# Column sums of the gates by products with ones, and an earlier hand-over from plain to seven-product units

## Chip, cores, metric

One core of one Trainium2 chip. The metric is the time of one execution in microseconds on the device; lower is better. The core has TensorE (PE, matrix products; PEld is its weight load), VectorE (DVE), ScalarE (ACT), GpSimd (POOL) and SyncE (SP, which issues the transfers here). Each engine works its own instructions off in program order; semaphores join them.

## What is computed

```
x  = attention(q, k, v)                      # windowed and dilated heads, to (2304, 512)
P  = exp(x @ w_gate - max)                   # (2304, 8)
for _ in range(8):                           # Sinkhorn
    P /= P.sum(1, keepdims=True) + 1e-9      # over the 8 experts
    P /= P.sum(0, keepdims=True) + 1e-9      # over all 2304 tokens
    P *= 2304 / 8
for e in range(8):
    out += P[:, e:e+1] * (relu(x @ w1[e]) @ w2[e])     # 512 -> 1024 -> 512
h = out @ w_in                               # 512 -> 2048
g = where(h >= 1, h, where(h <= -1, 0, (h + 1)**2 / 4))
return g @ w_out
```

## The kernel before, in words

All factors of the large products are split into a high part (rounded by an ACT copy) and a low part (raw minus high, a DVE subtraction): `split`, lines 98 and 99. A product then is three matmuls (`product`, line 254): high by high, high by low, low by high.

The hidden columns of all experts and of the last feed-forward are cut into units of 512: 16 units of the experts (0 to 15) and 4 of the feed-forward (16 to 19). Tokens are cut into three passes of 768, each of two blocks of 384.

- **Unit 0** is plain: six blocks of 384 tokens, in the generator `first_unit`, whose steps are pulled between those of the attention. Blocks 4 and 5 run after the attention's end. A block has gate products (`gate_steps`), 16 steps of the first layer (12 yield "h", 4 yield "act") and 12 steps of the second ("y").
- **Units 1 to 19** are seven-product units: the first layer (`first_layer`) forms 2x2 blocks of weights and tokens by seven products in the order 1, 5, 6, 2, 7, 3, 4, each in two halves q (14 steps of six matmuls of 384 columns); the second layer (`second_layer`) has 24 steps of three matmuls of 512 columns. One unit on 768 tokens is called a run here. First all expert units run on pass 0, then 1, then 2; then the feed-forward's units in the same manner.

What prepares the next run is written as generators, pulled by hand at set steps of the layers:

- `prep_w1`: seven combinations of a unit's first weights. GpSimd forms sums (line 124), ACT and DVE split them into `w1o[i]`, and a transfer keeps each (line 118). For pass 0 the next unit's are made in the second layer; later passes load them (`load_steps`).
- `prep_w2`: loads four pieces of the second weights into a staging tile `raw2` (line 145), splits them into `w2o`. Pulled at the start of its own run, one piece at every second step of the first layer.
- `build_x`: the seven combinations of a pass's tokens: GpSimd subtracts (line 229) into t1 to t4, ACT and DVE split into `xo[i]`. For unit 1 it is pulled in block 5; at later changes of pass, three times in the first layer and then at every third step of the second.
- `sinkhorn_steps`: normalises the gates `prob`. Sums over the experts on DVE; the maximum and the eight sums over tokens go over the partitions by GpSimd's `partition_all_reduce` (lines 676 and 690). Pulled in the run of unit 1 at every second step of the first layer and every fourth of the second.
- `double_steps`: converts the feed-forward's 64-bit weights on DVE from the first run of pass 1 on (lines 187 to 217).
- `turn_steps`: 24 transposes on TensorE that turn the experts' output into the feed-forward's tokens, one pass ahead, in the second layer from step 10 on (line 868); they use the PSUM banks "h" of the first layer's pa.

The activation of each finished half is in stages (`begin`, `move_on`): `act_relu` has two (ACT, then DVE line 376), `act_ffn` three (ACT line 855; DVE 851 and 852, then ACT 853; DVE 856).

```
        def begin(src, f, j):
            move_on()
            stages = act(src, f, j)
            stages.pop(0)()
            under_way.append(stages)
```

Of the kernel before, what the change touches and what calls it, by code (L numbers as in the profile page):

```python
# [18 lines left out]
P = 128  # L19
# [8 lines left out]
def tile_attention_moe_ffn(ctx: ExitStack, tc, q, k, v, w_gate, w1, w2, w_in, w_out, out):  # L28
# [63 lines left out]
    def split(raw, pair, eng, hi_on_dve=False):  # L92
# [5 lines left out]
            nc.scalar.activation(out=hi, in_=raw, func=AF.Copy)  # L98
        eng.tensor_tensor(out=lo, in0=raw, in1=hi.bitcast(F32), op=ALU.subtract)  # L99

    def words(t):
        return t.bitcast(F32)

# [5 lines left out]
    def prep_w1(u, raw, into, pause=0):  # L109

        (a11, a12), (a21, a22) = parts_of(raw)

        def made(i, src):
            o = into(i)
            for q in range(UQ):
                split(src[:, q], (o[:, 0, q], o[:, 1, q]), nc.vector)
                yield
            nc.sync.dma_start(out=w1_kept[u][i - 1], in_=words(o).rearrange("p h q c f -> p (h q c f)"))
            for _ in range(pause):
                yield  # L120
# [44 lines left out]
    def double_steps(scr, stage1, stage2):  # L165
# [13 lines left out]
            nc.sync.dma_start(out=raws[n % 2], in_=src)  # L179

        load(0)
        yield
        for n, (u, m, c) in enumerate(pieces):
            if n + 1 < len(pieces):
                load(n + 1)
# [36 lines left out]
    def build_x(k, free, eng, order):  # L222

        v = xf[:, k].rearrange("p (k c) (j x) -> p k j c x", k=2, j=2)
        b11, b12, b21, b22 = v[:, 0, 0], v[:, 0, 1], v[:, 1, 0], v[:, 1, 1]
        t1, t2, t3, t4 = free
        def subtract(out_, in0, in1):
            for o, x, y in zip(*(each(z) for z in (out_, in0, in1))) if isinstance(out_, list) else ((out_, in0, in1),):
                eng.tensor_tensor(out=o, in0=x, in1=y, op=ALU.subtract)  # L229

        subtract(t1, b12, b11)
        subtract(t2, b22, t1)
        subtract(t3, b22, b12)
        subtract(t4, b21, t2)
        yield
        of = {1: b11, 5: t1, 6: t2, 2: b21, 7: t3, 3: b22, 4: t4}
        for i in order:
            if isinstance(of[i], list):
                for c in range(2):
                    split(of[i][c], (xo[i][:, 0, c], xo[i][:, 1, c]), nc.vector)  # L240
            else:
                split(of[i], (xo[i][:, 0], xo[i][:, 1]), nc.vector)
            yield

    def each(x):
        return x if isinstance(x, list) else [x[:, 0], x[:, 1]]
# [10 lines left out]
    def first_layer(u, act, late):  # L257
# [20 lines left out]
                    under_way.remove(stages)  # L278

        def begin(src, f, j):  # L280
            move_on()
            stages = act(src, f, j)
            stages.pop(0)()
            under_way.append(stages)

        for i in ORDER:
# [383 lines left out]
                                in_=pt.rearrange("p (t s e) -> p t e s", t=TPH, s=2), axis=AX.X, op=ALU.add)  # L670

    def sinkhorn_steps(pool):
        m = pool.tile([P, 1], F32, name="gmax")
        nc.vector.tensor_reduce(out=m, in_=prob, axis=AX.XY, op=ALU.max)
        mm = pool.tile([P, 1], F32, name="gmax_all")
        nc.gpsimd.partition_all_reduce(mm, m, P, bass.bass_isa.ReduceOp.max)
        yield
        nc.vector.tensor_scalar(out=prob, in0=prob, scalar1=mm, scalar2=None, op0=ALU.subtract)
        nc.scalar.activation(out=prob, in_=prob, func=AF.Exp)
        rows = pool.tile([P, NTILE], F32, name="rows")  # L680
        cols = pool.tile([P, E], F32, name="cols")
        call = pool.tile([P, E], F32, name="call")
        for _ in range(N_ITER):
# [3 lines left out]
            nc.vector.tensor_tensor(out=prob, in0=prob, in1=rows.unsqueeze(2).to_broadcast([P, NTILE, E]),  # L687
                                    op=ALU.mult)
            nc.vector.tensor_reduce(out=cols, in_=prob.rearrange("p t e -> p e t"), axis=AX.X, op=ALU.add)
            nc.gpsimd.partition_all_reduce(call, cols, P, bass.bass_isa.ReduceOp.add)  # L690
            yield
            nc.vector.tensor_scalar(out=call, in0=call, scalar1=1e-9, scalar2=None, op0=ALU.add)
            nc.vector.reciprocal(out=call, in_=call)
            nc.vector.tensor_scalar(out=call, in0=call, scalar1=float(NT) / E, scalar2=None, op0=ALU.mult)
            nc.vector.tensor_tensor(out=prob, in0=prob, in1=call.unsqueeze(1).to_broadcast([P, NTILE, E]),
# [11 lines left out]
    with tc.manual_schedule():  # L707
# [114 lines left out]
        at.h = hs  # L822
        raw = stage1()
        nc.sync.dma_start(out=raw, in_=unit_sources(1)[0])
        free = [[late.tile([P, HALF], F32, tag=f"kept{n}", bufs=2, name=f"t{n}") for _ in range(2)] for n in range(3)]
        x4 = stage2()
        free.append([x4[:, c, :HALF] for c in range(2)])
        build = build_x(0, free, nc.gpsimd, (5, 6, 1, 2, 7, 3, 4))
        nxt = prep_w1(1, raw, lambda i: w1o[i])
        made = 0  # L830
        for s in moe:
            if at.block < NB - 1:
                continue
            if at.part != "y":
                if s == "act":
                    pull(build)
            else:
                pull(nxt)
                made += 1
                if made <= 3:  # L840
                    pull(build)
        drain(build)
        drain(nxt)
# [1 line left out]
        def act_ffn(src, f, j):  # L845
            at_ = slice(j * HALF, (j + 1) * HALF)
            hi, lo = hs[0][:, f, at_], hs[1][:, f, at_]
            r = late.tile([P, HALF], F32, tag="r", bufs=2, name="r")

            def middle():  # L850
                nc.vector.scalar_tensor_tensor(out=r, in0=r, scalar=1.0, in1=r, op0=ALU.min, op1=ALU.mult)  # L851
                nc.vector.tensor_tensor(out=r, in0=r, in1=src, op=ALU.max)  # L852
                nc.scalar.activation(out=hi, in_=r, func=AF.Copy)  # L853

            return [lambda: nc.scalar.activation(out=r, in_=src, func=AF.Relu, bias=half, scale=0.5), middle,
                    lambda: nc.vector.tensor_tensor(out=lo, in0=r, in1=hi.bitcast(F32), op=ALU.subtract)]  # L856

        def finish_out(py, t):
            nc.vector.tensor_tensor(out=acc[:, t, :], in0=py, in1=acc[:, t, :], op=ALU.add)
# [15 lines left out]
                load_w1(u, i)  # L875
                yield

        sink = sinkhorn_steps(late)
        double = iter(())
        runs = ([(u, k) for k in range(NPASS) for u in range(1, N_MOE)]  # L880
                + [(u, k) for k in range(NPASS) for u in range(N_MOE, NU)])
# [8 lines left out]
        for n, (u, k) in enumerate(runs):  # L890
# [7 lines left out]
                finish = finish_add if u == 1 else finish_scaled(u)  # L898
            if n == N_MOE - 1:
                double = double_steps(xf[:, 0].rearrange("p c x -> p (c x)"), stage1, stage2)  # L900
            prep2 = prep_w2(u, stage2) if kind == "moe" and k == 0 else iter(())
            pull(prep2)
            turn = build = nxt = iter(())
            fresh = u2 is not None and k2 == 0 and units[u2][0] == "moe"
            if fresh:
# [15 lines left out]
            for m, i in enumerate(first_layer(u, act, late)):  # L921
                if m % 2 == 0:
                    pull(prep2)
                if not fresh and m % 2:
                    pull(nxt)
                if moves and m > 6 and m % 2 == 0:
                    pull(build)
                if u == 1 and k == 0 and m % 2:
                    pull(sink)
                if m % 2:  # L930
                    pull(double)
# [1 line left out]
            if not fresh:  # L933
                drain(nxt)
            for m, s in enumerate(second_layer(k, finish)):
                if fresh:
                    pull(nxt)
                if moves and m % 3 == 0:
                    pull(build)
                if m % 4 == 2:  # L940
                    pull(sink)
                if m % 3:
                    pull(double)
                if m > 9:
                    pull(turn)
            drain(nxt)
            drain(build)
# [33 lines left out]
```

## Time and profile before

| what | value |
|---|---|
| median of 3 runs | 2090.63 us (2090.07 to 2091.47) |
| profiled execution, its own time | 2088.01 us |
| profiled execution, its span | 2086.2 us |
| mean granted clock of TensorE | 0.984 of full speed |
| TensorE busy | 2008.3 us (96% of the span) |
| VectorE, ScalarE, GpSimd busy | 1190.4, 768.6, 234.1 us |

The span is from the first to the last instruction. An idle time stands in brackets behind the instruction that ended it, with the engine, tile and line that released it; "issue" means that the profile shows nothing that was waited for.

### The profile page before, as it was taken

What the parts mean: (1) busy time and instruction counts of PE and PEld (TensorE: products, weight loads), DVE (VectorE), ACT (ScalarE), POOL (GpSimd) and SP (SyncE); (2) the same over time, 40 slices, a digit from 0 to 9 for tenths busy, and PEclk for the clock granted to TensorE, in tenths of its full rate; (3) what the DMA queues carried; (4) which work ended last, traced back from release to release, by engine and by line L of the source; (5) the groups of instructions that cost most, each with busy time, mean ns of one, the idle gap of its engine ahead of it and who ended that gap; (6) DMA issues with size and microseconds to landing.
All of it is one profiled execution on the core that took longest, in us unless ns stands there. A gap on an engine that the chain in (4) does not pass through costs nothing.

```text
span 2086.2 us, 28892 instructions
## 1 busy us (share of the span) xinstructions
PE 2008.3 (96%) x10746; PEld 1806.6 (87%) x10746; DVE 1190.4 (57%) x2331; ACT 768.6 (37%) x1807; POOL 234.1 (11%) x269
## 2 busy tenths in 40 slices
PE   7999848999999999999999999999999999899999
PEld 6888738899899989899989989989989988798798
DVE  6644446666676665575575685633433356565756
ACT  5655415444444433223223234212212343443443
POOL 4213112221221300000002000000000100101000
PEclk9999978999999999999999999999999999999999
DMA  7431226666666666676667667645545545364552
GB/s 172 103 70 39 111 91 242 263 263 241 258 267 233 258 245 256 226 275 262 237 247 282 239 235 291 233 166 217 199 150 206 195 148 213 114 250 163 201 201 92
DMA packets 167499, 425.27 MB, mean 204 GB/s; under 512 B 78528, under 2 KB 78528, under 8 KB 160064
## 3 DMA queue, kind: packets, MB, share of 16 engines
q1 hardware_dynamic: 167360, 423.43, 55.9%
q8 instruction: 85, 1.39, 0.3%
q14 instruction: 54, 0.44, 0.1%
HBM read 309.08 MB, written 114.29 MB: 203 GB/s over the span
## 4 chain that ended last, share of the span: by engine, by line
PE 88%; DVE 6%; ACT 2%; issue 2%; DMA 1%; POOL 0%; SPq 0%; POOLq 0%; DVEq 0%; ACTq 0%
PE py L254 44%; PE pa L254 21%; PE pc L254 11%; PE pb L254 5%; PE ph L254 3%; PE s L527 2%; DVE xo L99 1%; PE px L569 1%; DVE r L852 1%; DVE r L851 1%; DVE hl L856 1%; ACT hh L853 1%; PE pt L495 1%; PE pe L553 1%; DVE kept L272 0%
## 5 line engine op out<-in xcount | busy, mean ns | idle before, releaser
L254 PE MATMUL py<-w2o,hh 128*128 128x512 f32 x2736 | 846.2, 390 | 0.5 <-DVE kept L272 0.5
L254 PEld LDWEIGHTS py<-w2o,hh 128*128 128x128 f32 x2736 | 511.9, 188 | 102.0 <-DVE kept L272 1.4
L254 PE MATMUL py<-w2o,hl 128*128 128x512 f32 x1368 | 533.5, 390 | 3.0 <-DVE hl L856 3.0
L254 PE MATMUL pa<-xo,w1o 128*128 128x384 f32 x2736 | 518.9, 337 | 16.7 <-DVE kept L272 12.0
L254 PEld LDWEIGHTS pa<-xo,w1o 128*128 128x128 f32 x2736 | 483.6, 189 | 23.6 <-DVE kept L272 13.6
L269 ACT ACTIVATE kept<-pa 128x384 f32<-128x384 f32 x228 | 111.7, 490 | 551.5 <-PE pa L254 549.9
L392 DVE SCALAR_TENSOR_TENSOR acc<-py,prob,acc 128x512 f32<-128x512 f32 x252 | 178.5, 750 | 231.8 <-PE py L254 227.1
L254 PEld LDWEIGHTS py<-w2o,hl 128*128 128x128 f32 x1368 | 257.1, 188 | 58.4 <-DVE hl L856 4.9
L254 PE MATMUL pc<-xo,w1o 128*128 128x384 f32 x1368 | 257.9, 336 | 33.0 <-DVE acc L383 31.0
L254 PEld LDWEIGHTS pc<-xo,w1o 128*128 128x128 f32 x1368 | 240.1, 189 | 34.4 <-issue 31.3
L124 POOL TENSOR_TENSOR raw<-raw 128x256 f32<-128x256 f32 x152 | 132.7, 902 | 867.6 <-DVE raw L205 374.8
L375 ACT ACTIVATE hh<-kept 128x384 fp32r<-128x384 f32 x270 | 141.9, 526 | 196.9 <-DVE kept L272 196.9
L272 DVE TENSOR_TENSOR kept<-pb,kept 128x384 f32<-128x384 f32 x114 | 63.3, 556 | 237.7 <-PE pb L254 237.6
L376 DVE SCALAR_TENSOR_TENSOR hl<-kept,hh 128x384 fp32r<-128x384 f32 x270 | 149.9, 555 | 4.2
L254 PE MATMUL pb<-xo,w1o 128*128 128x384 f32 x684 | 128.7, 336 | 0.0
L99 DVE TENSOR_TENSOR w1o<-raw,w1o 128x256 fp32r<-128x256 f32 x210 | 99.5, 518 | 47.7 <-ACT w1o L98 47.7
L254 PEld LDWEIGHTS pb<-xo,w1o 128*128 128x128 f32 x684 | 120.5, 189 | 0.0
L98 ACT ACTIVATE w1o<-raw 128x256 fp32r<-128x256 f32 x210 | 76.6, 415 | 90.4 <-POOL raw L124 90.4
L229 POOL TENSOR_TENSOR xf<-xf 128x768 f32<-128x768 f32 x20 | 37.1, 1875 | 631.8 <-ACT xf L870 629.3
L853 ACT ACTIVATE hh<-r 128x384 fp32r<-128x384 f32 x96 | 50.4, 525 | 129.8 <-DVE r L852 129.8
L99 DVE TENSOR_TENSOR w2o<-raw,w2o 128x512 fp32r<-128x512 f32 x60 | 43.0, 716 | 81.2 <-ACT w2o L98 81.2
L269 ACT ACTIVATE kept<-pc 128x384 f32<-128x384 f32 x114 | 56.1, 492 | 55.7 <-PE pc L254 55.3
(131 smaller groups left out, 1683.0 us busy)
## 6 DMA issues: line engine op xcount, KB each, us to landing
w1o<-w_kept SPq DMA_DIRECT2D x294, 512.0 KB, 5.9
w2o<-w_kept SPq DMA_DIRECT2D x42, 2048.0 KB, 7.9
w_kept<-w1o SPq DMA_DIRECT2D x105, 512.0 KB, 3.4
w_kept<-w2o SPq DMA_DIRECT2D x15, 2048.0 KB, 6.3
raw<-in_moe_w_dram SPq DMA_DIRECT2D x15, 1024.0 KB, 7.2
raw<-in_moe_w_dram SPq DMA_DIRECT2D x60, 256.0 KB, 3.4
w_kept<-raw SPq DMA_DIRECT2D x28, 512.0 KB, 2.9
xf<-in_moe_w_in_dram SPq DMA_DIRECT2D x16, 512.0 KB, 5.0
```

Of the source, the lines that this page charges most:

```text
L98: nc.scalar.activation(out=hi, in_=raw, func=AF.Copy)
L99: eng.tensor_tensor(out=lo, in0=raw, in1=hi.bitcast(F32), op=ALU.subtract)
L124: nc.gpsimd.tensor_tensor(out=out[:, q], in0=in0[:, q], in1=in1[:, q], op=op)
L229: eng.tensor_tensor(out=o, in0=x, in1=y, op=ALU.subtract)
L254: nc.tensor.matmul(o, lhsT=a(h), rhs=b(l), start=first and n == 0, stop=last and n == 2, skip_group_check=on)
L269: nc.scalar.activation(out=dst, in_=src, func=AF.Copy)
L272: nc.vector.tensor_tensor(out=dst, in0=src, in1=dst, op=ALU.add)
L375: return [lambda: nc.scalar.activation(out=hi, in_=src, func=AF.Relu), lambda: nc.vector.scalar_tensor_tensor(out=lo, in0=src, scalar=0.0, ...
L376: lambda: nc.vector.scalar_tensor_tensor(out=lo, in0=src, scalar=0.0, in1=hi.bitcast(F32), op0=ALU.max, op1=ALU.subtract)]
L392: nc.vector.scalar_tensor_tensor(out=acc[:, t, :], in0=py, scalar=prob[:, t, e:e + 1], in1=acc[:, t, :], op0=ALU.mult, op1=ALU.add)
L527: nc.tensor.matmul(s[:, i, :], lhsT=qd[:, pr, j, :], rhs=kt[:, pr, key0(j):key0(j) + KW], start=not early, stop=not early or i == JG - 1)
L853: nc.scalar.activation(out=hi, in_=r, func=AF.Copy)
```

## The change

The two sums over partitions are made by TensorE: a tile of ones as weights, the column sums as the moving operand, the result read from PSUM by DVE; the maximum by a product with the identity and a broadcast with a row of ones. Each product is emitted two pulls after its operand. The normalisation now begins in block 5 of unit 0, every second step from step 5 on, and ends in unit 1. The token combinations for unit 1 begin in block 4; their t4 has a tile of its own; the second weights of a run are requested at the start of the second layer of the run before. A split's DVE half is emitted one pull after its ACT half (`high`). At changes of pass `build_x` is pulled in the second layer alone, at every second step. The 64-bit conversion starts seven pulls later, its first load is issued when it was. Transposes start at step 12 instead of 10. `begin` emits the new half's ACT stage before older stages, and `act_ffn` writes its maximum over its source where that lies in SBUF.

```diff
+    def high(raw, pair):
+        hi, lo = pair
+        nc.scalar.activation(out=hi, in_=raw, func=AF.Copy)
+        return lambda: nc.vector.tensor_tensor(out=lo, in0=raw, in1=hi.bitcast(F32), op=ALU.subtract)
# prep_w1
-                split(src[:, q], (o[:, 0, q], o[:, 1, q]), nc.vector)
+                low = high(src[:, q], (o[:, 0, q], o[:, 1, q]))
                 yield
+                low()
# double_steps
         load(0)
-        yield
+        for _ in range(8):
+            yield
# build_x
-        subtract(t4, b21, t2)
+        if not callable(t4):
+            subtract(t4, b21, t2)
         yield
         of = {1: b11, 5: t1, 6: t2, 2: b21, 7: t3, 3: b22, 4: t4}
-        for i in order:
+        for n, i in enumerate(order):
+            if callable(t4) and n == 4:
+                of[4] = t4()
+                subtract(of[4], b21, t2)
             if isinstance(of[i], list):
-                for c in range(2):
-                    split(of[i][c], (xo[i][:, 0, c], xo[i][:, 1, c]), nc.vector)
+                lows = [high(of[i][c], (xo[i][:, 0, c], xo[i][:, 1, c])) for c in range(2)]
             else:
-                split(of[i], (xo[i][:, 0], xo[i][:, 1]), nc.vector)
+                lows = [high(of[i], (xo[i][:, 0], xo[i][:, 1]))]
             yield
+            for low in lows:
+                low()
# begin
-            move_on()
             stages = act(src, f, j)
             stages.pop(0)()
+            move_on()
             under_way.append(stages)
# sinkhorn_steps
+        ones = pool.tile([P, P], F32, name="ones")
+        nc.vector.memset(ones, 1.0)
...
-        nc.gpsimd.partition_all_reduce(mm, m, P, bass.bass_isa.ReduceOp.max)
         yield
-        nc.vector.tensor_scalar(out=prob, in0=prob, scalar1=mm, scalar2=None, op0=ALU.subtract)
+        yield
+        pm = bank(*at.sink, "pm")
+        nc.tensor.matmul(pm[:1, :P], lhsT=m, rhs=ident, start=True, stop=True)
+        one = pool.tile([1, 1], F32, name="one")
+        nc.vector.tensor_reduce(out=one, in_=pm[:1, :P], axis=AX.X, op=ALU.max)
+        yield
+        yield
+        nc.tensor.matmul(pm[:, P:P + 1], lhsT=ones[:1, :], rhs=one, start=True, stop=True)
+        nc.vector.tensor_copy(out=m, in_=pm[:, P:P + 1])
+        nc.vector.tensor_scalar(out=prob, in0=prob, scalar1=m, scalar2=None, op0=ALU.subtract)
         nc.scalar.activation(out=prob, in_=prob, func=AF.Exp)
+        yield
...
-            nc.gpsimd.partition_all_reduce(call, cols, P, bass.bass_isa.ReduceOp.add)
             yield
-            nc.vector.tensor_scalar(out=call, in0=call, scalar1=1e-9, scalar2=None, op0=ALU.add)
+            yield
+            pc = bank(*at.sink, "psum")[:, :E]
+            nc.tensor.matmul(pc, lhsT=ones, rhs=cols, start=True, stop=True)
+            nc.vector.tensor_scalar(out=call, in0=pc, scalar1=1e-9, scalar2=None, op0=ALU.add)
# hand-over from unit 0 to unit 1
-        x4 = stage2()
-        free.append([x4[:, c, :HALF] for c in range(2)])
+        ahead = prep_w2(1, stage2)
+        pull(ahead)
+        free = [pair("kept0"), pair("kept1"), pair("kept2"), lambda: pair("r")]
...
+        at.sink = ("s", 1)
+        made = turns = 0
         for s in moe:
-            if at.block < NB - 1:
-                continue
-            if at.part != "y":
-                if s == "act":
+            if at.block == NB - 1 and s != "gate" and s != "x":
+                turns += 1
+                if turns > 4 and turns % 2:
+                    pull(sink)
+            if at.block == NB - 2 and s == "y":
+                made += 1
+                if made % 2 and made < 10:
                     pull(build)
-            else:
+            elif at.block == NB - 1 and s == "y":
+                made += 1
                 pull(nxt)
-                made += 1
-                if made <= 3:
+                if made <= 14:
                     pull(build)
# act_ffn
+            g = r if src.space == PSUM else src
...
-                nc.vector.tensor_tensor(out=r, in0=r, in1=src, op=ALU.max)
-                nc.scalar.activation(out=hi, in_=r, func=AF.Copy)
+                nc.vector.tensor_tensor(out=g, in0=r, in1=src, op=ALU.max)
+                nc.scalar.activation(out=hi, in_=g, func=AF.Copy)
# the loop over runs
-            prep2 = prep_w2(u, stage2) if kind == "moe" and k == 0 else iter(())
-            pull(prep2)
+            prep2, ahead = ahead, iter(())
...
-                if moves and m > 6 and m % 2 == 0:
-                    pull(build)
-                if u == 1 and k == 0 and m % 2:
+                if k == 0 and u < 3 and m % 2:
+                    at.sink = ("y", 2)
                     pull(sink)
...
             for m, s in enumerate(second_layer(k, finish)):
+                if fresh and m == 0:
+                    ahead = prep_w2(u2, stage2)
+                    pull(ahead)
                 if fresh:
                     pull(nxt)
-                if moves and m % 3 == 0:
+                if moves and m % 2:
                     pull(build)
-                if m % 4 == 2:
+                if m > 5 and m % 2:
+                    at.sink = ("h", 2)
                     pull(sink)
...
-                if m > 9:
+                if m > 11:
                     pull(turn)
```

## Rows read from the trace of the kernel before

**Rows 1.** Timeline of PE: first product of several runs (start, us, then the instruction).

```profile
238.95 2.26 PE L254 MATMUL pa<-xo,w1o 128*128 128x384 f32 x12
...
286.21 2.27 PE L254 MATMUL pa<-xo,w1o 128*128 128x384 f32 x12
...
351.08 2.27 PE L254 MATMUL pa<-xo,w1o 128*128 128x384 f32 x12
...
381.99 2.27 PE L254 MATMUL pa<-xo,w1o 128*128 128x384 f32 x12
...
1749.05 2.27 PE L254 MATMUL pa<-xo,w1o 128*128 128x384 f32 x12
...
1853.73 2.27 PE L254 MATMUL pa<-xo,w1o 128*128 128x384 f32 x12
```

**Rows 2.** Timeline of PE: instructions before which it stood idle.

```profile
249.64 2.29 PE L254 MATMUL pa<-xo,w1o 128*128 128x384 f32 x6 [4.30 <-ACT kept L269]
...
319.51 4.18 PE L254 MATMUL pc<-xo,w1o 128*128 128x384 f32 x12 [31.03 <-DVE acc L383]
...
1772.79 0.55 PE L868 MATMUL p<-ident,acc 128*128 128x128 f32 x3 [1.51 <-DVE r L852]
...
1801.43 1.32 PE L254 MATMUL pa<-xo,w1o 128*128 128x384 f32 x6 [2.08 <-DVE kept L272]
```

**Rows 3.** Waits of the whole trace: us in total, times, longest.

```profile
POOL raw L124 <- issue: 21.4, 3, 7.5
...
POOL call L690 <- issue: 11.5, 2, 5.8
...
DVE xf L187 <- DMA xf<-in_moe_w_in_dram: 10.6, 2, 10.2
```

**Rows 4.** Timeline of POOL, around the long wait, and in a later unit.

```profile
284.12 1.43 POOL L124 TENSOR_TENSOR raw<-raw 128x256 f32<-128x256 f32 x2 [6.86 <-issue]
291.36 0.43 POOL L690 PARTITION_ALL_REDUCE call<-cols  x1 [5.81 <-issue]
...
430.86 5.67 POOL L124 TENSOR_TENSOR raw<-raw 128x256 f32<-128x256 f32 x6 [14.32 <-DVE w1o L99]
```

**Rows 5.** Timeline of DVE: low halves of splits; first and last operation of one round.

```profile
235.69 0.95 DVE L99 TENSOR_TENSOR xo<-xf,xo 128x768 fp32r<-128x768 f32 x1
236.57 1.75 DVE L99 TENSOR_TENSOR w1o<-raw,w1o 128x256 fp32r<-128x256 f32 x5
...
256.24 0.16 DVE L692 TENSOR_SCALAR call<-call 128x8 f32<-128x8 f32 x1
...
258.42 0.44 DVE L689 TENSOR_REDUCE cols<-prob 128x8 f32<-128x144 f32 x1
```

**Rows 6.** Chain that ended last, around the hand-over: a block's second layer; a load.

```profile
211.84 8.65 PE py L254 x36
...
245.14 3.41 DMA raw<-in_moe_w_dram
```

**Rows 7.** Windows: length, busy us of PE, PEld, DVE, ACT, POOL; clock; DMA; GB/s.

```profile
630.00:660.00 30.00, 30.00 (x153) 27.24 (x152) 19.53 (x38) 13.91 (x32) 7.57 (x8) 1.00 0.67 253
750.00:780.00 30.00, 28.19 (x138) 25.66 (x137) 17.39 (x34) 6.80 (x14) 1.05 (x2) 0.94 0.68 250
1200.00:1230.00 30.00, 30.00 (x152) 27.20 (x152) 27.28 (x47) 12.01 (x21) 1.79 (x2) 1.00 0.70 254
...
1800.00:1830.00 30.00, 25.90 (x120) 21.37 (x121) 21.24 (x35) 12.96 (x23) 0.00 (x0) 1.00 0.27 94
```

**Rows 8.** Timeline of PE: three plain fp32 products of 96 columns, two records each.

```profile
100.19 0.80 PE L527 MATMUL s<-kt,qd 128*128 128x96 f32 x6
```

**Rows 9.** Chain in the feed-forward: an activation's end, transposes, and a split.

```profile
1773.33 0.56 DVE hl L856
...
1776.24 0.33 PE p L868 x3
...
1799.19 0.74 ACT xo L98
```

More of the change, by code (lines that the diff above doesn't have):

```diff
@@ L672, in sinkhorn_steps @@
     def sinkhorn_steps(pool):
+        ones = pool.tile([P, P], F32, name="ones")
+        nc.vector.memset(ones, 1.0)
         m = pool.tile([P, 1], F32, name="gmax")
         nc.vector.tensor_reduce(out=m, in_=prob, axis=AX.XY, op=ALU.max)
-        mm = pool.tile([P, 1], F32, name="gmax_all")
-        nc.gpsimd.partition_all_reduce(mm, m, P, bass.bass_isa.ReduceOp.max)
         yield
-        nc.vector.tensor_scalar(out=prob, in0=prob, scalar1=mm, scalar2=None, op0=ALU.subtract)
+        yield
[8 more added lines that the diff above has]
+        nc.vector.tensor_scalar(out=prob, in0=prob, scalar1=m, scalar2=None, op0=ALU.subtract)
         nc.scalar.activation(out=prob, in_=prob, func=AF.Exp)
+        yield
         rows = pool.tile([P, NTILE], F32, name="rows")
@@ L824, in tile_attention_moe_ffn, with pair @@
         nc.sync.dma_start(out=raw, in_=unit_sources(1)[0])
-        free = [[late.tile([P, HALF], F32, tag=f"kept{n}", bufs=2, name=f"t{n}") for _ in range(2)] for n in range(3)]
-        x4 = stage2()
-        free.append([x4[:, c, :HALF] for c in range(2)])
+        ahead = prep_w2(1, stage2)
+        pull(ahead)
+        def pair(tag):
+            return [late.tile([P, HALF], F32, tag=tag, bufs=2, name="t") for _ in range(2)]
+        free = [pair("kept0"), pair("kept1"), pair("kept2"), lambda: pair("r")]
         build = build_x(0, free, nc.gpsimd, (5, 6, 1, 2, 7, 3, 4))
         nxt = prep_w1(1, raw, lambda i: w1o[i])
-        made = 0
+        sink = sinkhorn_steps(late)
+        at.sink = ("s", 1)
+        made = turns = 0
         for s in moe:
-            if at.block < NB - 1:
-                continue
-            if at.part != "y":
-                if s == "act":
+            if at.block == NB - 1 and s != "gate" and s != "x":
[5 more added lines that the diff above has]
+                if made % 2 and made < 10:
                     pull(build)
-            else:
+            elif at.block == NB - 1 and s == "y":
+                made += 1
                 pull(nxt)
-                made += 1
-                if made <= 3:
+                if made <= 14:
                     pull(build)
@@ L848, in act_ffn @@
             r = late.tile([P, HALF], F32, tag="r", bufs=2, name="r")
+            g = r if src.space == PSUM else src
             def middle():
                 nc.vector.scalar_tensor_tensor(out=r, in0=r, scalar=1.0, in1=r, op0=ALU.min, op1=ALU.mult)
-                nc.vector.tensor_tensor(out=r, in0=r, in1=src, op=ALU.max)
-                nc.scalar.activation(out=hi, in_=r, func=AF.Copy)
+                nc.vector.tensor_tensor(out=g, in0=r, in1=src, op=ALU.max)
+                nc.scalar.activation(out=hi, in_=g, func=AF.Copy)
             return [lambda: nc.scalar.activation(out=r, in_=src, func=AF.Relu, bias=half, scale=0.5), middle,
-                    lambda: nc.vector.tensor_tensor(out=lo, in0=r, in1=hi.bitcast(F32), op=ALU.subtract)]
+                    lambda: nc.vector.tensor_tensor(out=lo, in0=g, in1=hi.bitcast(F32), op=ALU.subtract)]
         def finish_out(py, t):
@@ L876, in load_steps @@
                 yield
-        sink = sinkhorn_steps(late)
         double = iter(())
```

## The prediction

> **What bounds the kernel now.** I first lay the starts of the runs side by side [rows 1]. An undisturbed run takes 381.99 - 351.08 = 30.91 us; the windows of such a run show PE busy for 30.00 of 30.00 us [rows 7]. TensorE is the bound there, and no other engine's saving is worth anything. So what can be won is what single runs take above 30.91. Unit 1 takes 286.21 - 238.95 = 47.26, a loss of 16.35. Unit 2 takes 351.08 - 286.21 = 64.87, a loss of 33.96. The window around the first run of pass 1 has PE idle for 1.81 us and a clock of 0.94 [rows 7], a loss of 1.81 + 0.06 x 30 = 3.6. The three feed-forward runs from 1749.05 to 1853.73 take 104.68; less 3 x 30.91 and eight groups of transposes of 0.33 [rows 9], 9.3 are lost, and the same pattern stands once more, two in all: 18.7. Together 50.3 + 3.6 + 18.7 = 72.6 us.
>
> Next I read what ended PE's idle times [rows 2]. The longest, 31.03, ended with a DVE addition, but DVE was only the last link. GpSimd has two kinds of work there in turn: the sums of unit 2's weights and the all-reduces of the gates. Each change of kind comes after 5.8 to 6.9 us in which the profile shows nothing waited for [rows 4]. In the whole trace this happens before sums three times, 21.4 us, and before all-reduces twice, 11.5 [rows 3]; a later unit's six sums run without it, after an ordinary wait for DVE [rows 4]. So it is the alternation that costs. After it PE is slow as well: the twelve matmuls behind the 31 us take 4.18 [rows 2], those of an undisturbed run 2.27 [rows 1], half the speed.
>
> **The change part by part, the all-reduces first.** Without them GpSimd has one kind of work, and I see no row that would leave any of the 32.9 us standing. The sums of unit 2 then wait for splits alone, as in the later unit. The long idle goes whole, and with it the slow stretch behind it.
>
> [...]
>
> What is added: ten products on PE. The nearest row is a plain fp32 product of 96 columns, 0.80 us for three [rows 8], 0.27 each: 2.7 us. Eight columns instead of 96 may cost less (nothing is the lower end), one product alone between others more; the upper end is 0.55, which a group of three transposes took behind an idle [rows 2], for each product: 5.5. I take 2.7, as the product row is the nearest in kind.
>
> **What the products make PE wait for.** PE works in order. A product waits for the column sums of its round, which stand in DVE's queue behind whatever was emitted earlier, and the matmuls behind it wait too. One round on DVE (four operations up to the new gates, five to the next sums) lasts from 256.24 to 258.86, 2.6 us [rows 5]. In block 5's second layer a round is pulled every four steps, which PE does in 4 x 8.65 / 12 = 2.9 [rows 6]. In that time DVE also has four low halves of weights at 1.75 / 5 = 0.35 [rows 5], so 4.0 against 2.9. From the start of that layer to product 5 of unit 1 DVE has: three rounds, 7.8; twelve of unit 1's low halves, 4.2; four token combinations at 0.95 (2, 7, 3, 4), 3.8; the last activation, 0.56: 16.4. PE offers 8.65 and product 1, 2.26 [rows 1]: 10.9. The missing 5.5 are waited for by the second and third product and by product 5, which needs the low half of weight 5. Some of DVE's work is past its deadline only in part, and I take 4.5 (bounds: 0 if all the lows slip into gaps, and 5.5).
>
> The rest of unit 1 carries five rounds, 13.0 us. An ordinary run of pass 0 has DVE busy for 19.5 of 30 [rows 7], so about 10.8 of 30.91 are free: 2.2 are over. Two more weight pieces must be loaded there (3.41 each from request to arrival [rows 6]), and ACT, which also empties PSUM, stands in front of them. I add a wait of 1 for each and take 4.2 in all (bounds 0 and 10, if both loads and each of five rounds held PE for 1 to 2 us).
>
> Each of these waits is short, but a low clock may follow: the idle of 1.81 us in rows 7 cost as much again in clock, while the 2.08 in the feed-forward [rows 2] lie in a window of clock 1.00 [rows 7]. I take one such stretch, 1.8. Sum left of 50.3: 2.7 + 4.5 + 4.2 + 1.8 = 13.2; won 37.1.
>
> **The earlier hand-over.** The 4.30 us before product 6 [rows 2] ended with an ACT copy that stood behind the split of a weight piece whose load was requested late (chain, [rows 6]). The first two loads now go out before block 4, so this wait is gone; it lies within the 37.1. The token combinations moved into block 4 find GpSimd, ACT and DVE with room: PE ran 8.65 us there without a wait for them [rows 6]. t4 moves past the sums on GpSimd's queue and costs 2 subtractions ahead of them, hidden as product 4 is the last. SP now has two loads ahead of the weight stores in each pass-0 run; PE waits for neither in an undisturbed run, so nothing.
>
> **Start of pass 1.** DVE waited 10.2 us for the 64-bit weights' first load [rows 3], and additions behind it held PE. The load is issued when it was, its use comes seven pulls later, over a first layer of 30.91 less 24 steps of 8.65 / 12, 13.6 us: the wait is covered. Were it not, 3.6 would stay. Against that, the seven pulls and the splits now crowd the second layer of later runs; at the next change of pass DVE was busy for 27.28 of 30 [rows 7]. I count 0.2 for it and win 3.4 (bounds 1.6 and 3.6).
>
> **Feed-forward.** The 2.08 us [rows 2] come from tokens' splits pulled between activations in the first layer: DVE takes a low half only after ACT's copy, 0.74 [rows 9] and 0.95 [rows 5], 1.7 for each of three. These pulls are now behind all activations, and DVE no longer waits for the copy. The transposes waited 1.51 for the bank that the last activation read; two steps later is 1.4 by rows 6, so the first wait goes and the second group still waits about 1.2: the last-but-one activation ends at 1773.89 [rows 9] and the last a whole one later. In the next run the last activation ends some 26 us after the start (the last but one after 1773.89 - 1749.05 = 24.8 in this one); seven lows and six additions, some 10 us, follow, so additions that free the PSUM banks end after the next run's start, and product 5 waits about 0.9. I leave 2.7 of 9.3 at each change, with the clock's share, and win 13.2 for both (bounds 8 and 17). The order in `begin` alone I cost at nothing: DVE's order is as before, and the ACT copy it delays is behind DVE work either way.
>
> **Sum.** 37.1 + 3.4 + 13.2 = 53.7. The profiled execution's own time is 2088.0 (its span and 1.8 around it), so 2034.3; the median of the runs shown lies 2.6 above it, so 2036.9 for a median. I give 2036.
>
> **The rivals.** *All hidden*: DVE's rounds fall into gaps and only the products remain. Left are 2.7 and some 2 of the feed-forward: 72.6 - 4.7 = 68, 2023. For it speaks that waits on DVE can overlap each other; against it the 16.4 where PE offers 10.9.
>
> *VectorE becomes the bound of the hand-over*: the waits reach their bounds, 5.5 + 10 instead of 8.7, and the products 5.5: 10 more, 2046. For it speaks that PE now stands behind DVE eight times, where only DVE stood behind GpSimd.
>
> *Many short idles, each with a slow stretch*: seven waits, of which I counted one with 1.8; six more cost 10.8, 2047. The row for it is the 1.81 with its 0.94, the row against it the 2.08. [...]
>
> *The change doesn't do what it says*: the idle before GpSimd's sums belongs to the sums. Then unit 2's loss of 33.96 stays: 2036 + 34 = 2070. The later unit's row speaks against it.
>
> *Slower*: in the feed-forward's 12 runs ACT's new order delays each activation. A run has eight in a chain; the last-but-one now ends those 24.8 us after the run's start and is used by step 18 of the second layer, 13.6 + 18 x 0.72 = 26.6 after it. So 1.8 / 7 = 0.26 for each activation is free, and beyond it a run loses seven times the excess. The 53.7 won are lost over 12 runs at 4.5 each, 0.64 for each activation more: from 0.9 on for each activation the kernel is slower, e.g. at 1.0 by 0.1 x 7 x 12 = 8, 2099. That is more than an ACT copy's whole length, and nothing on ACT is moved by more than one.
>
> **How the numbers follow.** Differences under 0.2% (4 us) are about what a measurement of this kernel can't tell from no change. Forecast 0.60 (its own range 2028 to 2043), all hidden 0.14, VectorE 0.13, clock 0.07, not what it says 0.03, slower 0.02, the remaining 0.01 for gains that cancel. Faster therefore 0.97, same 0.01, slower 0.02. The range takes in the forecast, the greater part of all hidden and the two cases near 2047: 2021 to 2049.
>
> **What would show it.** No PARTITION_ALL_REDUCE, and no idle of GpSimd above 5 us that ends with "issue"; unit 2 at 31 us; unit 1 between 35 and 44, its waits named after DVE's column sums and w1o's low halves; no wait of DVE for the 64-bit load; in the feed-forward no wait of pa for DVE, and transposes with one wait of about 1.2. Wrong it would be if PE's idle between block 5 and unit 2 exceeded 20 us, if unit 2's sums still waited on "issue", or if an undisturbed run no longer took 30.91.

## The result and the profile after

The changed kernel took 2041.18 us (median of four runs, 2039.7 to 2047.63) against 2090.86 for the kernel before: a ratio of 0.977, 95% interval 0.975 to 0.979. The profiled execution has a span of 2037.8 us, 48.4 less than before, and the time lies in the range that was given (2021 to 2049), 5 us above the 2036 that was forecast.

Where the 48.4 came from is read by the starts of the runs, as in [rows 1]. I use the gate products of block 5 as the beginning of the hand-over (220.33 us in the trace before, 219.29 in the one after) and the first product of unit 3 as its end. The third stage ends with the first product of the second run of pass 1 (788.12 before).

| stage | before | after | won | forecast |
|---|---|---|---|---|
| up to block 5's gates | 220.33 | 219.29 | 1.0 | 0 |
| hand-over: block 5 to unit 3 | 130.75 | 99.68 | 31.1 | 37.1 |
| unit 3 to the second run of pass 1 | 437.04 | 432.99 | 4.1 | 3.4 |
| from there to the end | 1298.08 | 1285.84 | 12.2 | 13.2 |

An undisturbed hand-over would take 80.44: 18.62 for block 5 as in the kernel before (its first product of unit 1 [rows 1] less 220.33) and two runs of 30.91. So 19.2 us are left in it. The 1.0 of the first row isn't put down to the change: in the twelve kernels below block 5 begins between 217.2 and 221.8 us, so whole executions differ by up to 4.6 us before the hand-over begins, and stage times are the safer comparison.

The timeline of PE in the changed kernel (start, us, then the instruction, in brackets the idle time before it and who ended it) answers to [rows 1, 2]:

```profile
232.66 0.28 PE L717 MATMUL psum<-cols,ones 128*128 128x8 f32 x2
232.79 0.71 PE L267 MATMUL py<-w1o,hh 128*128 128x512 f32 x2
...
236.78 0.39 PE L717 MATMUL psum<-cols,ones 128*128 128x8 f32 x2 [0.95 <-DVE cols L713]
...
241.01 0.39 PE L717 MATMUL psum<-cols,ones 128*128 128x8 f32 x2 [0.94 <-DVE cols L713]
...
247.27 1.32 PE L267 MATMUL pc<-xo,w1o 128*128 128x384 f32 x6 [2.63 <-DVE w1o L105]
249.41 1.65 PE L267 MATMUL pc<-xo,w1o 128*128 128x384 f32 x4 [0.81 <-DVE w1o L105]
...
251.14 4.19 PE L267 MATMUL pa<-xo,w1o 128*128 128x384 f32 x12
...
260.09 1.31 PE L267 MATMUL pa<-xo,w1o 128*128 128x384 f32 x6 [0.97 <-ACT kept L282]
...
266.19 0.55 PE L717 MATMUL psum<-cols,ones 128*128 128x8 f32 x2 [2.71 <-DVE cols L713]
...
279.53 0.39 PE L717 MATMUL psum<-cols,ones 128*128 128x8 f32 x2 [0.74 <-DVE cols L713]
...
288.06 2.27 PE L267 MATMUL pa<-xo,w1o 128*128 128x384 f32 x12
...
318.97 2.27 PE L267 MATMUL pa<-xo,w1o 128*128 128x384 f32 x12
```

The 31 us idle is gone, and unit 2 takes 318.97 - 288.06 = 30.91. In its place stand seven waits, 9.75 us together, all but one for DVE: four for products' column sums, two for the low half of weight 5. The twelve matmuls at 251.14 take 4.19 instead of the 2.27 at 288.06: a slow stretch (granted clock 0.50) lies from 249.2 to 256.0, from the end of the fourth wait on, and a second one from 266.3 to 269.7, behind the 2.71. Two windows (columns as in [rows 7]) give their share:

```profile
240.00:260.00 20.00, 14.72 (x64) 13.54 (x63) 13.52 (x36) 7.87 (x19) 5.41 (x7) 0.83 0.59 221
260.00:280.00 20.00, 16.47 (x73) 14.38 (x74) 18.06 (x52) 9.04 (x23) 4.41 (x6) 0.91 0.56 210
```

GpSimd's timeline in the same stretch has only sums, and what each waits for is data ([rows 4] before):

```profile
241.43 3.99 POOL L131 TENSOR_TENSOR raw<-raw 128x256 f32<-128x256 f32 x5 [2.48 <-DVE w1o L105]
258.47 1.42 POOL L131 TENSOR_TENSOR raw<-raw 128x256 f32<-128x256 f32 x2 [13.04 <-DMA raw<-in_moe_w_dram]
275.59 4.91 POOL L131 TENSOR_TENSOR raw<-raw 128x256 f32<-128x256 f32 x6 [15.71 <-DVE w1o L105]
```

At the start of pass 1 PE has no wait left; at a change of pass in the feed-forward it has two:

```profile
1738.64 0.55 PE L903 MATMUL p<-ident,acc 128*128 128x128 f32 x3 [0.96 <-DVE r L887]
...
1782.42 2.35 PE L267 MATMUL pc<-xo,w1o 128*128 128x384 f32 x12 [1.31 <-ACT kept L282]
```

The name behind the 1.31 must be read with care: that ACT copy was over at 1781.70, as the chain shows, and PE began 0.72 later. DVE's timeline shows what came last, the additions that empty product 5's banks, behind seven low halves:

```profile
1774.95 5.30 DVE L105 TENSOR_TENSOR xo<-xf,xo 128x768 fp32r<-128x768 f32 x6 [0.18 <-ACT xo L104]
1780.17 0.68 DVE L894 TENSOR_TENSOR acc<-py,acc 128x512 f32<-128x512 f32 x1
1780.77 0.95 DVE L105 TENSOR_TENSOR xo<-xf,xo 128x768 fp32r<-128x768 f32 x1
1781.63 3.07 DVE L894 TENSOR_TENSOR acc<-py,acc 128x512 f32<-128x512 f32 x5
```

### The profile page after: what moved, and what is told of

Its sections match the earlier page's. It is cut to its first block, busy times and chain, and to the rows that moved or that the text cites. A ratio compares the mean times of both kernels' runs of the same rounds, so it can differ in the third digit from the quotient of the medians.

```text
span 2037.8 us, 29040 instructions
## 1 busy us (share of the span) xinstructions
PE 2004.4 (98%) x10766; PEld 1805.7 (89%) x10766; DVE 1189.2 (58%) x2334; ACT 774.2 (38%) x1807; POOL 226.5 (11%) x260
## 4 chain that ended last, share of the span: by engine, by line
PE 94%; DVE 3%; ACT 1%; DMA 1%; issue 0%; POOL 0%; SPq 0%; POOLq 0%; DVEq 0%; ACTq 0%
PE py L267 47%; PE pa L267 23%; PE pc L267 11%; PE pb L267 6%; PE ph L267 3%; PE s L540 2%; PE px L582 1%; PE pe L566 1%; PE pt L508 1%; DMA raw<-in_moe_w_dram 1%; PE pg L672 0%; DVE hl L891 0%; DVE r L886 0%; PE p L903 0%; ACT hh L888 0%
## 5 line engine op out<-in xcount | busy, mean ns | idle before, releaser
L388 ACT ACTIVATE hh<-kept 128x384 fp32r<-128x384 f32 x270 | 142.0, 526 | 176.6 <-DVE kept L285 176.0
L267 PE MATMUL ph<-xo,w1o 128*128 128x384 f32 x288 | 66.4, 356 | 0.0
## 6 DMA issues: line engine op xcount, KB each, us to landing
raw<-in_moe_w_dram SPq DMA_DIRECT2D x60, 256.0 KB, 5.7
```

What stands on the lines that cost most here:

```text
L267: nc.tensor.matmul(o, lhsT=a(h), rhs=b(l), start=first and n == 0, stop=last and n == 2, skip_group_check=on)
L388: return [lambda: nc.scalar.activation(out=hi, in_=src, func=AF.Relu), lambda: nc.vector.scalar_tensor_tensor(out=lo, in0=src, scalar=0.0, ...
```

## The experiments

Twelve kernels. Stage times are read as in the table above; a time without an interval is one execution.

**Products alone.** The kernel before with the products in place of the all-reduces, at the old pulls (shown for the sum; the maximum likewise).

```diff
-            nc.gpsimd.partition_all_reduce(call, cols, P, bass.bass_isa.ReduceOp.add)
             yield
+            pc = bank(*at.sink, "psum")[:, :E]
+            nc.tensor.matmul(pc, lhsT=ones, rhs=cols, start=True, stop=True)
```

> The kernel before with the products with ones alone, one pull after their operands, pulled where the all-reduces were. Theory (GpSimd's change between all-reduces and sums is what cost): the idle of 31.03 us and the slow stretch behind it go, unit 2 takes 31 to 33 us instead of 64.87, unit 1 stays near 45, and the time is about 2088 - 33 = 2055. Rival (the earlier schedule is what pays, since the sums of unit 2 were late for their splits): unit 2 still takes over 50 us and the time is above 2075.

Measured: 2064.34 us, hand-over 106.3. PE's timeline:

```profile
238.87 2.26 PE L254 MATMUL pa<-xo,w1o 128*128 128x384 f32 x12
...
250.10 0.59 PE L680 MATMUL pm<-ident,gmax 128*1 128x128 f32 x2 [6.43 <-DVE gmax L677]
...
295.65 2.27 PE L254 MATMUL pa<-xo,w1o 128*128 128x384 f32 x12
...
326.56 2.27 PE L254 MATMUL pa<-xo,w1o 128*128 128x384 f32 x12
```

Unit 2 takes 30.91 instead of 64.87, as the theory said. But unit 1 takes 56.78, 9.5 more than before and not the 45 that I expected: the first product waits 6.43 us for a maximum that stands in DVE's queue behind the late weight piece of [rows 6]. What held DVE alone now holds PE.

**Sums on VectorE, all-reduces kept.** The kernel before; only unit 2's sums move.

```diff
-                nc.gpsimd.tensor_tensor(out=out[:, q], in0=in0[:, q], in1=in1[:, q], op=op)
+                (nc.vector if u == 2 else nc.gpsimd).tensor_tensor(out=out[:, q], in0=in0[:, q], in1=in1[:, q], op=op)
```

> The kernel before with its nine all-reduces, but the sums of unit 2's weights are made by VectorE instead of GpSimd, so that GpSimd has all-reduces alone between unit 1's and unit 3's sums. Theory (the change of kind costs, not the all-reduce): no idle of GpSimd ends with issue between 255 and 320 us, unit 2 takes 31 to 33 us, the time is about 2055. Rival (the all-reduces or the chain through GpSimd are slow by themselves): unit 2 keeps most of its loss of 34, the time is above 2080.

Measured: 2061.34, hand-over 103.7. All nine all-reduces are still there. The last of them and what follows, in GpSimd's timeline, and unit 2 in PE's:

```profile
285.83 0.50 POOL L690 PARTITION_ALL_REDUCE call<-cols  x1 [4.03 <-DVE cols L689]
299.65 1.44 POOL L124 TENSOR_TENSOR raw<-raw 128x256 f32<-128x256 f32 x2 [13.32 <-DMA raw<-in_moe_w_dram]
```

```profile
285.96 2.27 PE L254 MATMUL pa<-xo,w1o 128*128 128x384 f32 x12
...
291.63 4.18 PE L254 MATMUL pc<-xo,w1o 128*128 128x384 f32 x12 [3.40 <-DVE acc L383]
...
323.89 2.27 PE L254 MATMUL pa<-xo,w1o 128*128 128x384 f32 x12
```

No idle on "issue" is left, and unit 2 falls from 64.87 to 37.93. That is more than the 31 to 33 expected; 7 remain, a wait for the chain of additions on DVE and its slow stretch. So the all-reduce was never the price; its neighbours of another kind were.

**All-reduces back.** The changed kernel with them: each is issued right behind its operand, and its result is used where the product stood (shown for the sum).

```diff
+            nc.gpsimd.partition_all_reduce(call, cols, P, bass.bass_isa.ReduceOp.add)
             yield
             yield
-            pc = bank(*at.sink, "psum")[:, :E]
-            nc.tensor.matmul(pc, lhsT=ones, rhs=cols, start=True, stop=True)
...
```

> The changed kernel with the all-reduces back in place of the products, at the same pulls. Theory (change of kind): between the normalisation's start in block 5 and its end in unit 1's second layer GpSimd changes between sums and all-reduces some six times at 5.6 to 7.5 us, PE loses 25 to 45 us more than in the changed kernel, the time is 2065 to 2085. Rival (the schedule pays): within 5 us of 2041.

Measured: 2079.64, hand-over 142.0, more than in the kernel before. GpSimd:

```profile
244.17 0.43 POOL L707 PARTITION_ALL_REDUCE call<-cols  x1 [5.85 <-issue]
251.57 1.40 POOL L131 TENSOR_TENSOR raw<-raw 128x256 f32<-128x256 f32 x2 [6.97 <-issue]
258.76 0.43 POOL L707 PARTITION_ALL_REDUCE call<-cols  x1 [5.79 <-issue]
266.17 4.40 POOL L131 TENSOR_TENSOR raw<-raw 128x256 f32<-128x256 f32 x6 [6.98 <-issue]
```

So the earlier start by itself doesn't pay: with it the all-reduces stand among unit 1's sums as well.

**Normalisation later.** The changed kernel, nothing pulled in block 5.

```diff
-                if turns > 4 and turns % 2:
-                    pull(sink)
+                pass
```

> The changed kernel with no pull of the normalisation in block 5: it starts in unit 1 and ends in unit 2's first layer. Theory (VectorE's queue is crowded around the end of block 5): the four waits there, 0.95, 0.94, 2.63 and 0.81 us, go and at least one of the two slow stretches with them, 5 to 9 us, so 2032 to 2036. Rival (each product makes PE wait wherever it stands): the waits appear again in units 1 and 2, the time stays at 2039 to 2043.

Measured: 2036.89, ratio 0.9745 (0.9728 to 0.9761); hand-over 95.9. The four waits fell from 5.33 us to 0.50, but seven others make 8.1, the longest for a copy behind the third weight piece:

```profile
254.18 1.98 PE L267 MATMUL pa<-xo,w1o 128*128 128x384 f32 x6 [3.61 <-ACT kept L282]
```

Both sides were half right: of the 3.8 us won in the stage 1.2 are waiting, and the rest is clock (0.50 for 3.4 us here, for 10.2 in the changed kernel). The interval overlaps that of the changed kernel.

**The 1 MB load behind the weight pieces**, in the changed kernel, for unit 1 alone.

```diff
-                nc.sync.dma_start(out=raw, in_=unit_sources(u2)[0])
+                if n:
+                    nc.sync.dma_start(out=raw, in_=unit_sources(u2)[0])
...
+                if n == 0 and m == 4:
+                    nc.sync.dma_start(out=raw, in_=unit_sources(u2)[0])
```

> The changed kernel with the 1 MB load of unit 2's first weights requested at step 4 of unit 1's first layer, behind the third and fourth piece of unit 1's second weights instead of ahead of them. Theory (the third piece waits behind the 1 MB on the same DMA engines, ACT and VectorE stand behind it): ACT's wait of 5.1 us for the piece falls below 4, the sixth product's wait of 2.71 us falls below 1.5, 2 to 4 us won, 2037 to 2039. Rival (the piece waits for VectorE's low halves, not for the 1 MB): the waits stay, 2041; or unit 2's sums come late and unit 2 takes more than 31 us.

Measured: 2038.28, ratio 0.9758 (0.9740 to 0.9777); hand-over 96.7. ACT's wait for the piece fell from 5.1 to 2.1, PE's 0.97 went, but the product's 2.71 only to 2.41. Unit 2 stayed at 30.91. The time is the one expected, the reason mostly another. SyncE's timeline, first in the changed kernel, then here:

```profile
250.47 2.44 SPq L940 DMA_DIRECT2D raw<-in_moe_w_dram  x1
252.99 0.98 SPq L152 DMA_DIRECT2D raw<-in_moe_w_dram  x2
```

```profile
251.44 1.90 SPq L152 DMA_DIRECT2D raw<-in_moe_w_dram  x2
```

Issuing the 1 MB load held SyncE's queue for 2.44 us, and the third piece was requested only behind it. Counted from unit 1's start (242.04, here 242.82) the request now comes 2.3 earlier; the transfer itself fell only from 6.0 to 5.2. Why the issue took so long there isn't shown; the same load of the next unit took 0.40.

**Both together.**

> Both: no pull of the normalisation in block 5, and the 1 MB load behind the pieces. Theory (the two causes are separate): the gains add, PE's idle between block 5 and unit 2 falls below 4 us, no slow stretch, 2028 to 2034. Rival (waits move on to unit 2): no faster than the better of the two alone.

Measured: 2035.12, ratio 0.9737 (0.9722 to 0.9752); hand-over 93.2. PE's idle was 6.9 us in nine waits of 0.35 to 1.55, not under 4, but none was followed by a slow stretch. In the stage the gains add, 3.8 and 3.0 alone and 6.5 together; the time lies 1 above the range expected, and its interval overlaps those of the two alone. The window of the stage, first in the changed kernel, then here:

```profile
235.00:320.00 85.00, 75.25 (x351) 66.43 (x350) 64.90 (x156) 36.31 (x83) 17.79 (x22) 0.94 0.65 242
```

```profile
235.00:320.00 85.00, 78.01 (x386) 67.34 (x385) 67.09 (x172) 40.51 (x94) 21.33 (x24) 1.00 0.66 243
```

**Token combinations in the first layer again**, in the changed kernel.

```diff
+                if moves and m > 6 and m % 2 == 0:
+                    pull(build)
...
-                if moves and m % 2:
+                if moves and m % 3 == 0:
                     pull(build)
```

> The changed kernel with the token combinations pulled as before at changes of pass: three times in the first layer, then at every third step of the second. Theory (splits between activations held VectorE): in the last feed-forward run of a pass PE waits again for VectorE before product 4, 1 to 2 us, and in the second layer, so 2 to 5 us for each of two changes, 2045 to 2050. Rival (the deferred low halves alone mended it): no such wait, 2041.

Measured: 2039.08. My theory failed here: no wait of product 4 came back, and the 1.31 of product 5 went too. Three feed-forward runs from the last of a pass on take 93.13 us (1749.32 to 1842.45), against 94.30 in the changed kernel.

**Low halves at once.** The changed kernel with the DVE half right behind the ACT half.

```diff
-        return lambda: nc.vector.tensor_tensor(out=lo, in0=raw, in1=hi.bitcast(F32), op=ALU.subtract)
+        nc.vector.tensor_tensor(out=lo, in0=raw, in1=hi.bitcast(F32), op=ALU.subtract)
+        return lambda: None
```

> The changed kernel with each low half emitted right behind its high half again, all pulls where they are. Theory (the place of the pulls pays, the deferral little): feed-forward within 1 us, hand-over up to 3 us slower, 2041 to 2044. Rival (the deferral mended the feed-forward): 8 us or more lost there, above 2049.

Measured: 2038.54; the same three runs take 94.28 (1746.47 to 1840.75). Hand-over 98.5. So undoing this edit alone costs nothing in the feed-forward either.

**Both of these undone.** That left two readings: each is enough, or neither does it.

> The changed kernel with both edits undone that showed no loss when undone alone: token combinations pulled in the first layer again, and low halves right behind their high halves. Theory (each of the two is enough): now product 4 of the last feed-forward run of a pass waits again for VectorE, about 2 us, and this run and the next lose 4 to 6 us for each of two changes of pass, 2046 to 2052. Rival (neither did it, but the new order in begin): run 19 stays at 30.91, 2041.

Measured: 2047.55; the three runs take 97.40 (1749.24 to 1846.64), 3.1 more than in the changed kernel at each of two changes. PE's timeline has the old waits:

```profile
1764.49 1.32 PE L268 MATMUL pa<-xo,w1o 128*128 128x384 f32 x6 [1.53 <-DVE kept L286]
...
1777.47 0.50 PE L268 MATMUL py<-w2o,hl 128*128 128x512 f32 x1 [0.98 <-DVE hl L892]
...
1786.82 2.35 PE L268 MATMUL pc<-xo,w1o 128*128 128x384 f32 x12 [0.96 <-DVE acc L895]
```

Each of the two is enough. The rest of the old loss shows in the chain: here the split follows the activation's copy at once,

```profile
1761.71 0.53 ACT hh L889
1762.24 0.74 ACT xo L104
1763.01 0.96 DVE xo L105
```

while in the kernel before the chain went through the next activation's first stage (ACT r, 0.51 us) between the two. The same three runs took 98.98 there (1785.65 to 1884.63), 1.6 more: three such links are 1.5. By these chains that is what the order in `begin` buys when the splits lie in the first layer; no kernel here undoes all three together.

**Old order in `begin`**, all else changed.

```diff
+            move_on()
             stages = act(src, f, j)
             stages.pop(0)()
-            move_on()
             under_way.append(stages)
```

> The changed kernel with older stages moved on before the new half's first stage again. Theory (VectorE's order is the same either way): undisturbed feed-forward runs stay at 30.91 us, waits in the last run of a pass change by under 0.5 us, the time is within 2 us of 2041. Rival (the order frees VectorE): the transposes' wait grows by 1 us or more, or product 4 waits again, 2044 or more.

Measured: 2042.72; the first transposes wait 0.16 and product 5 1.52 instead of 1.31; as expected.

**Conversion and transposes early again.**

```diff
-        for _ in range(8):
-            yield
+        yield
...
-                if m > 11:
+                if m > 9:
                     pull(turn)
```

> The changed kernel with two edits undone that lie in separate stages: the 64-bit conversion starts one pull after its first load again, and the transposes at step 10 again. Theory: VectorE waits about 10 us for the load in the first run of pass 1 and PE loses 2 to 4 us there; the first transposes wait 1.0 to 1.5 us in each of two passes; together 4 to 7, 2045 to 2048. Rival (one or the other was hidden by the remaining edits): that stage shows no wait.

Measured: 2050.37, above the range. The two stages answer as expected, PE's timeline:

```profile
737.97 3.70 PE L266 MATMUL pa<-xo,w1o 128*128 128x384 f32 x12 [2.10 <-DVE kept L284]
...
1742.56 0.55 PE L902 MATMUL p<-ident,acc 128*128 128x128 f32 x3 [1.32 <-DVE r L886]
```

The first run of pass 1 takes 34.88 (723.20 to 758.08), 4.0 more; the run with the transposes 36.42 instead of 35.04. With two of those that is 6.7; the rest of the 9 lies in the hand-over (101.0, 1.3 more) and in another slow stretch at a change of pass (three transposes at 1875.49 take 0.90 instead of the 0.49 of 1879.06).

**What helped, together, column sums three pulls behind.**

```diff
         yield
-        yield
         nc.tensor.matmul(pm[:, P:P + 1], lhsT=ones[:1, :], rhs=one, start=True, stop=True)
...
+            yield
             yield
             yield
             pc = bank(*at.sink, "psum")[:, :E]
...
-                if m > 5 and m % 2:
+                if m > 3 and m % 2:
                     at.sink = ("h", 2)
```

with the edits of "both together" and "token combinations in the first layer again".

> The changed kernel with all that helped: the normalisation starts in unit 1 and each product stands three pulls behind its operand instead of two, the 1 MB load behind the pieces, and the token combinations pulled in the first layer too (with deferred low halves). Theory (the products' waits come from their distance to VectorE's queue): the waits for column sums fall from 4.9 us to under 2, the two waits of product 5 at 1.3 after each change of pass go, 2029 to 2033. Rival (VectorE's total work bounds units 1 and 2): the waits move on to later products or to product 5, 2034 to 2036.

Measured: 2031.11 (median of five), ratio 0.9723 (0.9707 to 0.9738), the fastest; its interval lies below the changed kernel's 0.9747. The hand-over, though, takes 93.7, no less than the 93.2 of "both together". The waits for column sums fell from 4.9 to 2.95, not under 2, and others came.

```profile
249.54 0.38 PE L698 MATMUL pm<-one,ones 1*128 1x1 f32 x2 [2.42 <-DVE one L696]
...
271.75 0.39 PE L717 MATMUL psum<-cols,ones 128*128 128x8 f32 x2 [2.18 <-DVE cols L712]
...
292.32 2.36 PE L267 MATMUL pa<-xo,w1o 128*128 128x384 f32 x12 [1.23 <-DVE kept L285]
```

The time lies in the theory's range, but not for its reason. The run doesn't settle theory against rival either, as its edit does two things: the column sums got a third pull, while the broadcast of the maximum was left with one instead of two (the first lines of the diff), and the longest wait, 2.42, is that broadcast's; "both together" has none there. Behind the 2.18 a slow stretch follows (clock 0.50 from 272.7 to 276.1), which "both together" doesn't have. What the profiled execution won over that of "both together" is 1.2 us of the feed-forward at each change of pass, and 3.05 us ahead of block 5 (218.71 against 221.76), where the two kernels do the same work; the latter is no gain of the edits.

## Why the prediction was right

**The long idle.** Right, in cause and in size. Three experiments agree: without all-reduces unit 2 is whole (products alone), with all-reduces but without sums between them most of the loss is gone (sums on VectorE), and with more changes of kind than before it is worse (all-reduces back; the waits on "issue" there are seven, 28.7 us ahead of sums and 17.7 ahead of all-reduces). The trace also holds a step that I had not seen: at each change of kind GpSimd's sequencer has a pair of MODIFY_POOL_CONFIG. The timeline leaves it out; the view of a source line shows it, here for the kernel before:

```profile
L676 POOLq MODIFY_POOL_CONFIG  x2: 8/8/8, 243.1 to 243.1; - x2
L690 POOLq MODIFY_POOL_CONFIG  x4: 1/1/1, 285.8 to 300.5; - x4
L124 POOLq MODIFY_POOL_CONFIG  x6: 88/108/108, 277.2 to 306.3; - x6
```

Those are six pairs for six changes. Five idle times on "issue" follow such a pair; the first pair lies in a wait for DVE. By GpSimd's timelines "all-reduces back" has ten changes of kind, seven of them with an idle time on "issue" and three within waits for data (19.97, 6.96 and 6.74 us); "sums on VectorE" has two, both within waits for data (6.93 and 13.32 us). The changed kernel has no all-reduce and no such pair behind the first microsecond. The idle times on "issue" are 5.6 to 7.5 us in the kernel before and 5.8 to 7.4 in "all-reduces back". What happens in them isn't shown: the runs show the change of kind as the condition and, in the kernel before, the MODIFY_POOL_CONFIG at it.

**The products.** Forecast 2.7 us for ten. Between neighbours the starts move by 0.13 (232.66 to 232.79, no wait) to 0.31 (0.46 for the one in the second slow stretch), ten together about 2.5. Right.

**PE behind VectorE.** Forecast 4.5 up to product 5 and 4.2 after; measured 0.95 + 0.94 + 2.63 + 0.81 = 5.3 and 0.97 + 2.71 + 0.74 = 4.4. Mechanism, places and sizes came out nearly as the queue's sum said, in this execution: in two kernels whose edits lie elsewhere ("token combinations in the first layer again", "conversion and transposes early again") the same three later waits sum to 5.5. The count of DVE's work against PE's offer was worth more than any single duration.

**The clock: the mis-sized term.** I counted one slow stretch at 1.8 us. Of the 19.2 us left, 9.75 are waits and 2.5 products; 7.0 remain. The two windows above lose 0.17 x 20 + 0.09 x 20 = 5.2 to the clock, in two stretches instead of one, the first twice as long; what the other 1.8 are isn't shown. Of the 6.0 us by which the hand-over fell short, 5.2 are this term with those 1.8 in it (7.0 against 1.8 forecast), and 1.0 the waits (9.75 against 8.7). So unit 1 took 46.0, above the 35 to 44 that were named as a sign. The rival of many short idles was therefore in part true: a slow stretch began at the end of four waits of 0.8 to 2.6 us, and another behind the 2.71. In the kernel with nine waits of 0.35 to 1.55, 6.9 us in all, none followed. So short idles alone don't decide it: the changed kernel has two stretches at 0.50 in its hand-over, and the one with nine waits a clock of 1.00 over the window from 235 to 320.

**The earlier loads.** The 4.30 of [rows 2] went; "products alone" shows what it becomes without them, 6.43. No kernel undoes the earlier loads alone. One thing I had passed over: a 1 MB load stands ahead of the third piece, as it did before, and ACT waited 5.1 us for the piece.

**Start of pass 1.** Forecast 3.4, measured 4.1; undone, 4.0 come back.

**Feed-forward.** Forecast 13.2, won 12.2, with the two waits that I named (about 1.2 and 0.9) at 0.96 and 1.31. The step on the cause was incomplete: I gave the credit to the place of the pulls and to the deferral together, while each is enough alone, and the place alone even costs 1.2 us at each change, because all seven low halves then stand ahead of the additions. `begin` was rightly costed at nothing in this kernel; by the chains it would be worth 1.6 us at a change of pass without the other two.

**The sum.** 53.7 us were forecast for the profiled execution, and 48.4 came: the hand-over fell short by 6.0 and the feed-forward by 1.0, the start of pass 1 gave 0.7 more. The 1.0 won ahead of block 5 was in no term; as far as the runs show it is luck.

## What to carry over

An engine's idle time that ends in nothing visible should be looked at for what kind of work came before and after it, and in the views of these lines for instructions that the timeline leaves out; here moving either kind away was the cure (unit 2 fell from 64.87 us to 30.91 and 37.93), and which one moved mattered little (2064.34 and 2061.34). A product that depends on a slow queue turned that queue's lateness into lateness of TensorE (6.43 us in "products alone"), so count all work that stands ahead of it there up to the deadline. Two edits that are each enough look useless when undone one at a time: undo both before giving credit.

## What the runs showed of the hardware that was not expected

In the kernel before and in "sums on VectorE", all-reduces that follow each other wait only for their data, 2.8 to 5.3 us of DVE's chain; the 5.6 to 7.5 us on "issue" came only between them and other GpSimd work, in two kernels, and in the kernel before behind a pair of MODIFY_POOL_CONFIG. A product of 8 columns in fp32 between other matmuls moved them by as little as 0.13 us.
